# Second layer by seven products: accumulating in two banks, 4 KB operand pieces, loads placed anew

## The chip, the cores and the metric

The kernel runs on one core of one Trainium2 chip. The metric is the device time of one execution in microseconds; the time before is the median of three runs.

## The reference

Performer attention of 8 x 8 heads (576 positions, head size 64, 128 features), then a mixing layer and a two-layer MLP on the 4608 rows of 512 columns:

```python
x = attention(q, k, v, omega)            # (8, 576, 512)
u = x + ((x.transpose(0, 2, 1) @ U) @ V).transpose(0, 2, 1)
out = u + np.maximum(u @ w_ch1, 0.0) @ w_ch2   # 512 -> 2048 -> 512
```

The change touches only the last line.

## The kernel before

All products are of fp32r halves: an operand is split into a high and a low part, and one product is three matmuls (high x high, high x low, low x high).

The attention and the mixing layer come first and leave `u` in `u_dram`. The MLP then goes over six chunks of 768 rows. Chunk 0 is multiplied plainly, under the end of the mixing layer. Chunk 1 takes its first layer by Strassen-Winograd (seven products of half-size blocks in place of eight) and its second layer plainly (`second`). Chunks 2 to 5 take both layers by seven products (`products2` and `Group`).

**The first layer.** The 2048 columns of `w_ch1` make 8 pairs p of two 128-column blocks. A pair has seven slots i; the slots of a chunk are counted n = 7p + i, from 0 to 55. In slot i, `product` (L1020) multiplies the split operand `slots[i]` of the chunk (sums and differences of its blocks) by the split weights of that product into bank X (even i) or Y (odd i), six matmuls of 128 x 384. X and Y of one pair are Y and X of the next. `after(i)` combines the banks on VectorE and ScalarE into the ReLU outputs and their sums, as seven operands T[1] to T[7] of the second layer; `less` (L1066) makes low parts and differences, `both` (L1076) splits two operands at once. Operations that may wait a little stand in the lists `due` and `pend`; `flush` runs them.

**The second layer.** Two pairs make a group of four per chunk. While a group's successor runs its first layer, the group's seven products of two halves j run in 14 steps s, one in each slot (`block`, L1289: six matmuls of 128 x 384). The order within a slot is fixed by hand:

```python
self.product(i, w, (X, Y))
evict, early_due = slot(i), len(due)    # slot(i) issues the block
after(i)
if i == 0 and pend:
    pend.pop(0)()
evict()
...                                      # operations due
lowers()                                 # low parts of the next chunk's operands
between(i)                               # loads, stores, next chunk
```

Products 1 and 6 stay in banks of their own over the chunk. Products 3, 2, 5, 7 and 4 start afresh in each group, in the bank `p_m` (j = 0) or `p_kv` (j = 1), and `evict` adds each to its sum (`sums`, L816), on VectorE. The order is `ORDER = (1, 3, 2, 6, 5, 7, 4)`. In the last group products 6, 7 and 4 run on in the bank of product 1, eight evictions go into sums (some banks are added twice), and GpSimd adds the sums of products 5, 6, 7 among each other in the group before it.

**The weights.** Chunk 1 stores the split operands of the first layer into `wx_dram` (`Weights`) and of the second into `w2x_dram` (`seconds`), and chunks 2 to 5 read them again: `Again.add` loads one operand of 256 KB (`wx`, 2 KB per partition) per slot, seven slots ahead, and `Group.load` one of 256 KB (`wy`) per slot.

**The next chunk.** `forward` fetches `u` of the next chunk into `uraw` (L376: pieces of 96 KB in runs of 128 bytes), `turn` transposes it on VectorE into free columns of `w1f` (L955), `prepare` makes the sums (L806), and `add` makes one operand of the slots: ScalarE the high part (L981), VectorE the low part (L806) in the `lowers` of the slot behind it. The last three operands and `prepare(4)` follow in the new chunk (`complete`: operands 5, 6, 7 at i = 0, 2, 4).

**Output.** `Output` transposes the four sums of the chunk before (`turn`, L1340, L1344), and `write` stores them (L1350: runs of 128 bytes).

Every operation of these stages is kept in program order on its engine and in its DMA queue; nearly all DMAs are issued by SP.

Of the kernel before, what the change touches and what calls it, by code (L numbers as in the profile page):

```python
# [29 lines left out]
def performer_mlp_kernel(ctx: ExitStack, tc, q, k, v, omega, U, V, w1, w2, out):  # L30
# [790 lines left out]

    def weight_tile():
        return up.tile([P, 2, 2, P], F32R, name="wx", bufs=8)

    w2x_dram = [dram.tile([P, 7, 2, 2 * P], F32, name=f"w2x_dram{p}") for p in range(NH)]
    wx_dram = [[dram.tile([P, 2, 2, P], F32, name=f"wx_dram{p}_{i}") for i in range(7)] for p in range(NH)]

    class Weights:
# [14 lines left out]
        def add(self):  # L843
# [15 lines left out]
            keep(nc.sync.dma_start(out=wx_dram[self.p][i], in_=f32(self.ops[-1])))  # L859

    class Again:


        def __init__(self, p):
            self.p, self.ops = p, []

        def add(self):
            i = len(self.ops)
            self.ops.append(weight_tile())
            keep(nc.sync.dma_start(out=f32(self.ops[-1]), in_=wx_dram[self.p][i]))  # L870

    def seconds(p):
# [8 lines left out]
            out=w2x_dram[p][:, i : i + n, h, :], in_=x.rearrange("p (n m) -> p n m", m=2 * P)  # L881
# [39 lines left out]
    class Chunk:  # L921
# [17 lines left out]
        def total(self, i):  # L939


            if self.c > 1:
                if i == 3:
                    return self.block(0, 1)
# [13 lines left out]
        def prepare(self, i):  # L958
# [7 lines left out]
            if self.c == 1 and i < 4:  # L966
# [49 lines left out]
        def product(self, i, w, banks):  # L1016
            o, x, wt = banks[i % 2], slots[i], w.ops[i]
# [7 lines left out]
        def products(self, p, w, between, steps, spread):  # L1025
# [24 lines left out]
            for i in range(7):  # L1050
                self.product(i, w, (X, Y))
# [6 lines left out]
        def products2(self, p, w, slot, between, pend):  # L1058
# [9 lines left out]
            def one(i, x):  # L1068
                T[i] = late["tl"].tile([P, 2, HT], F32R, name=f"t{i}", bufs=2)
# [43 lines left out]
            for i in range(7):  # L1113
                self.product(i, w, (X, Y))
# [36 lines left out]
        def residual(self, t):  # L1151
            if t in ((0, 1) if self.c else (2, 3)):
                self.u[t] = dec.tile([P, DM], F32, name="u", tag="de", bufs=2)
            elif self.c:
                self.u[t] = (dec if t < 4 else late["rp"]).tile([P, DM], F32, name="u", tag="mag" if t < 4 else "u", bufs=2)
            else:
                self.u[t] = (late["rp"] if t % 2 else dec).tile([P, DM], F32, name="u", tag="u" if t % 2 else "mag", bufs=2)
# [44 lines left out]
    def each(f, i):  # L1202
# [15 lines left out]
        if f == NF - 1:  # L1218
            pairs.add()
# [20 lines left out]
    ORDER = (1, 3, 2, 6, 5, 7, 4)  # L1240
# [12 lines left out]
    def make_acc():  # L1253
        places = [parted(w1f[:, r, 1408 : 1408 + HT]) for r in range(4)]
        places += [parted(late["rp"].tile([P, DM], F32, name="acc", tag="u", bufs=2)[:, :HT]) for _ in range(2)]
        places += [w1f[:, r, :].rearrange("p (a b) -> p a b", a=2)[:, :, 768 : 768 + HT // 2] for r in range(4)]
        for i, key in enumerate([(i, j) for i in (3, 5, 2, 4, 7) for j in range(2)]):
            acc[key] = places[i]

    class Group:  # L1260


        def __init__(self, chunk, g):
            self.chunk, self.g, self.T, self.w = chunk, g, [], {}

        def load(self):
            for k, i in enumerate(ORDER):
                for n in range(2):
                    w = self.w[i, n] = late["tr"].tile([P, 2, 2 * P], F32R, name="wy", bufs=8)
                    keep(nc.sync.dma_start(out=f32(w), in_=w2x_dram[2 * self.g + n][:, PLACE[i]]))  # L1270
                    yield

        def block(self, s):

            k, j = divmod(s, 2)
            i, res, last = ORDER[k], self.chunk.res, self.g == LAST
            key = 1 if last and i in (6, 7, 4) else i
            if key in (1, 6):
                if self.g == 0:
                    res[i, j] = ps.tile([P, HT], F32, name="p_r", tag="p_n" if i == 6 else "p_q", bufs=2)  # L1280
                bank = res[key, j]
            else:
                bank = ps.tile([P, HT], F32, name="p_o", tag="p_kv" if j else "p_m")
            more = key in (1, 6) and self.g > 0
            for n in range(2):
                w, x = self.w[i, n], self.T[n][i]
                js = slice(j * P, (j + 1) * P)
                for m, (l, r) in enumerate(passes((w[:, 0, js], w[:, 1, js]), (x[:, 0], x[:, 1]))):
                    keep(nc.tensor.matmul(  # L1289
                        bank, l, r, start=(n + m == 0 and not more), stop=(n == 1 and m == 2), skip_group_check=True,  # L1290
# [3 lines left out]
        def evict(self, i, j, bank):  # L1294
            chunk = self.chunk
            a = {n: acc[n, j] for n in (2, 3, 4, 5, 7)}
            if self.g == LAST:
                for n in {1: (2,), 6: (3,), 5: (3, 5), 7: (5,)}.get(i, (i,)):
                    sums(a[n], bank, a[n], ADD)
                return  # L1300
            if i == 1:
                return
            if i == 6:
                if self.g == LAST - 1:
                    chunk.f6[j] = parted(dec.tile([P, HT], F32, name="f6", tag="mag", bufs=2))
# [200 lines left out]
```

## Time and profile before

| | us |
|---|---|
| median of 3 runs | 1117.76 |
| lowest and highest run | 1117.25, 1119.66 |
| the profiled execution: its time | 1114.54 |
| its span, first to last instruction | 1112.8 |
| TensorE busy | 1052.9 (95%) |
| VectorE busy | 786.5 (71%) |
| ScalarE busy | 605.6 (54%) |
| GpSimd busy | 516.2 (46%) |

Busy time is the time in which an instruction of the engine runs. PE is TensorE's matmuls, PEld its weight loads, DVE VectorE, ACT ScalarE, POOL GpSimd, SP SyncE. A TensorE at half clock counts as busy. Times in the trace count from the span's start. The attention and mixing end at about 311 us, chunk 0 at 439, chunk 1 at 571, chunk 2 at 695, chunk 3 at 825, chunk 4 at 959, and the products of chunk 5 at 1084.

### The profile page before, as it was taken

How to read it: one execution, taken by the hardware profiler on the slowest of the kernel's cores; microseconds unless marked ns; L12 is line 12 of the kernel's file. 1: busy time of each engine (PE TensorE's matmuls, PEld its weight loads, DVE VectorE, ACT ScalarE, POOL GpSimd, SP SyncE). 2: the span in 40 equal slices, each digit the busy share in tenths (PEclk: the TensorE clock that was granted, in tenths of full speed). 3: DMA queues.
4: the chain of work that ended last, by engine and by line, in shares of the span. 5: the costliest groups of instructions: out<-in, count | busy, mean ns of one | idle time of the engine just before them, and what ended most of it. 6: DMA issues, size and time to landing. Idle time of an engine off the chain costs nothing.

```text
span 1112.8 us, 19650 instructions
## 1 busy us (share of the span) xinstructions
PE 1052.9 (95%) x6447; PEld 1002.8 (90%) x6447; DVE 786.5 (71%) x1519; ACT 605.6 (54%) x1513; POOL 516.2 (46%) x454
## 2 busy tenths in 40 slices
PE   9999999999999999899997999799989998899995
PEld 7999999999989998799887999799978998889994
DVE  4888998989877784656746567765586555875555
ACT  5899899898856553444335434434343443434330
POOL 3447457575545555478733324422272332722352
PEclk9999999999999999899998999899999998999998
DMA  9899897995144653689686899499986999779856
GB/s 137 143 164 166 175 183 117 221 142 106 47 161 133 161 114 114 208 264 285 227 284 232 272 248 296 155 274 287 248 249 198 285 259 228 241 229 290 266 199 133
DMA packets 420773, 226.47 MB, mean 204 GB/s; under 512 B 329792, under 2 KB 344128, under 8 KB 420672
## 3 DMA queue, kind: packets, MB, share of 16 engines
q1 hardware_dynamic: 411968, 224.14, 77.6%
q10 hardware_dynamic: 8704, 1.08, 0.7%
q8 instruction: 52, 0.85, 0.3%
q14 instruction: 49, 0.40, 0.1%
HBM read 176.91 MB, written 48.23 MB: 202 GB/s over the span
## 4 chain that ended last, share of the span: by engine, by line
PE 75%; DVE 12%; DMA 5%; ACT 3%; issue 2%; SPq 2%; POOL 1%; DVEq 0%; ACTq 0%; POOLq 0%
PE p_s L1020 22%; PE p_o L1289 10%; PE p_r L1289 6%; PE p_p L993 6%; PE p_n L532 4%; PE p_kv L486 4%; PE p_n L1139 3%; PE p_q L1139 3%; PE p_p L574 3%; PE p_q L512 2%; PE p_p L575 2%; PE p_p L576 2%; DVE ux L806 2%; PE py L346 2%; DMA uraw<-u_dram 2%
## 5 line engine op out<-in xcount | busy, mean ns | idle before, releaser
L1020 PE MATMUL p_s<-ux,wx 128*128 128x384 f32 x1680 | 350.9, 344 | 41.4 <-DVE t L1066 19.7
L1020 PEld LDWEIGHTS p_s<-ux,wx 128*128 128x128 f32 x1680 | 304.1, 193 | 55.4 <-DVE t L1066 22.4
L589 ACT ACTIVATE e<-p_p,nm 128x128 f32<-128x128 f32 x576 | 167.1, 389 | 23.8 <-DVE nm L582 15.5
L1289 PE MATMUL p_o<-t,wy 128*128 128x384 f32 x864 | 173.0, 335 | 0.7 <-DVE w1f L816 0.6
L816 POOL TENSOR_TENSOR near<-b,near 128x384 f32<-128x384 f32 x32 | 43.5, 1360 | 258.7 <-DVE near L1066 258.7
L1289 PEld LDWEIGHTS p_o<-t,wy 128*128 128x128 f32 x864 | 152.1, 188 | 1.4 <-DVE w1f L816 1.3
L436 POOL TENSOR_TENSOR xl<-xT,xh 128x384 fp32r<-128x384 f32 x95 | 94.1, 1009 | 112.4 <-ACT xh L432 94.3
L582 DVE TENSOR_REDUCE nm<-p_p 128x4 f32<-128x512 f32 x144 | 97.8, 680 | 22.6 <-PE p_p L576 14.3
L1076 ACT CAST t<-near 128x768 fp32r<-128x768 f32 x64 | 53.5, 836 | 97.7 <-DVE near L1066 71.3
L816 DVE TENSOR_TENSOR w1f<-p_o,w1f 128x384 f32<-128x384 f32 x112 | 61.1, 552 | 64.4 <-PE p_o L1289 64.2
L1289 PE MATMUL p_r<-t,wy 128*128 128x384 f32 x480 | 100.0, 346 | 0.0
L574 PE MATMUL p_p<-omh,xh 128*128 128x256 f32 x288 | 92.7, 322 | 1.1 <-ACT e L589 0.9
L1289 PEld LDWEIGHTS p_r<-t,wy 128*128 128x128 f32 x480 | 89.0, 197 | 0.0
L816 DVE TENSOR_TENSOR near<-p_s,near 128x384 f32<-128x384 f32 x88 | 48.5, 551 | 50.9 <-PE p_s L1020 50.7
L575 PE MATMUL p_p<-oml,xh 128*128 128x256 f32 x288 | 81.6, 283 | 0.0
L576 PE MATMUL p_p<-omh,xl 128*128 128x256 f32 x288 | 81.5, 284 | 0.0
L816 POOL TENSOR_TENSOR t<-near,t 128x768 fp32r<-128x768 f32 x32 | 59.3, 1854 | 30.6 <-ACT t L1076 30.6
L532 PE MATMUL p_n<-kv,eT 128*128 128x65 f32 x512 | 71.2, 269 | 0.1
L993 PE MATMUL p_p<-ux,wx 128*128 128x384 f32 x384 | 70.8, 336 | 0.0
L532 PEld LDWEIGHTS p_n<-kv,eT 128*128 128x128 f32 x512 | 67.1, 192 | 2.3 <-DVE x L557 0.3
L993 PEld LDWEIGHTS p_p<-ux,wx 128*128 128x128 f32 x384 | 67.6, 188 | 1.6
L486 PE MATMUL p_kv<-vt,e 128*128 128x65 f32 x480 | 66.3, 262 | 0.7 <-ACT e L589 0.7
(175 smaller groups left out, 2206.6 us busy)
## 6 DMA issues: line engine op xcount, KB each, us to landing
wx<-wx_dram SPq DMA_DIRECT2D x224, 256.0 KB, 4.6
wy<-w2x_dram SPq DMA_DIRECT2D x224, 256.0 KB, 4.3
raw<-in_moe_w_ch_dram SPq DMA_DIRECT2D x32, 512.0 KB, 4.1
wx_dram<-wx SPq DMA_DIRECT2D x56, 256.0 KB, 2.3
u_dram<-x SPq DMA_DIRECT2D x36, 256.0 KB, 2.2
qt<-in_q_dram SPq DMA_DIRECT2D x120, 72.0 KB, 3.1
uraw<-u_dram SPq DMA_DIRECT2D x80, 96.0 KB, 5.8
kt<-in_k_dram SPq DMA_DIRECT2D x52, 144.0 KB, 5.0
```

Of the source, the lines that this page charges most:

```text
L436: rest.tensor_tensor(out=self.xl[-1], in0=self.turned, in1=f32(self.xh[-1]), op=ALU.subtract)
L486: tc.keep_in_program_order(nc.tensor.matmul(o, e[:, j, :], w, start=(s == 0 and j == 0), stop=(s == NT - 1), skip_group_check=True))
L532: nc.tensor.matmul(pn[:, h, :], eT[:, h, :], kv[:, h, s // 5, :], start=True, stop=True)
L574: nc.tensor.matmul(o, part.xh[g][:, ts], oh, start=True, stop=False)
L575: nc.tensor.matmul(o, part.xh[g][:, ts], ol, start=False, stop=False)
L576: nc.tensor.matmul(o, part.xl[g][:, ts], oh, start=False, stop=True)
L582: nc.vector.tensor_reduce(out=self.nm[:, :n], in_=self.pp[:, :n], axis=AX.X, op=ALU.max, negate=True)
L589: nc.scalar.activation(out=self.e[:, j, :], in_=self.pp[:, j, :], func=AF.Exp, bias=self.nm[:, j : j + 1])
L816: keep(engine.tensor_tensor(out=out, in0=a, in1=b, op=op))
L993: keep(nc.tensor.matmul(ph, l, r, start=(cc + i == 0), stop=(cc == NC - 1 and i == 2)))
L1020: keep(nc.tensor.matmul(o, l, r, start=(i in (0, 1, 3) and k + j == 0), stop=(k == 1 and j == 2), skip_group_check=True,))
L1289: keep(nc.tensor.matmul(bank, l, r, start=(n + m == 0 and not more), stop=(n == 1 and m == 2), skip_group_check=True,))
```

## The change

- The order is `(1, 5, 2, 6, 3, 7, 4)`. Per half j, products 1, 6, 7 and 4 of a group go on accumulating in one bank (`p_q`) and products 5 and 3 in another (`p_m` or `p_kv`); product 2 stays in its bank (`p_n`) over the chunk. After each product but 2 the bank is added to one sum as it stands: after 1 to sum 2, after 6 to sum 3, after 7 and 5 to sum 5, after 3 to sum 3, after 4 to sum 4. Product 2 is added in the last group. The additions on GpSimd, the copies of products 6 and 7 and the double additions of the last group go. The first group adds the chunk's own blocks.
- The sums have new places, sum 5 two of them, used in turn by chunk.
- `wx_dram` is one tensor, from which two operands are loaded at once (`feed`: 512 KB, 4 KB per partition, every other slot, six slots ahead); `w2x_dram` holds both pairs of a group side by side, so that a `wy` load is 512 KB as well.
- `forward` begins at slot 20 in place of 30 and turns at 29, 33, 38, 42 in place of 36, 40, 44, 48; the first four operands are made at 50, 51, 52, 55 in place of 50, 52, 53, 55, the rest at 0, 1, 2 in place of 0, 2, 4; `prepare(4)` runs in slot 53 in place of slot 1, on GpSimd. In chunk 1 the operands of chunk 2 are made in slots 50 to 55, so that one is left.
- In chunk 1, chunk 0's stores come in slots 4 to 9, its seventh weights in slot 0, its last operand at i = 3. The first two residual tiles of chunk 1 have tag `uraw` in place of `de`.
- The output leaves as two tiles of 768 rows (sums 2 and 3) and four of 384 (sums 4 and 5), in other slots; at the end each sum is written when it is complete.

```diff
+    def weight_pair():
+        return up.tile([P, 2, 2, 2, P], F32R, name="wx", bufs=4)
...
-        return up.tile([P, 2, 2, P], F32R, name="wx", bufs=8)
+        if not halves:
+            pair = weight_pair()
+            halves.extend([pair[:, 0], pair[:, 1]])
+        return halves.pop(0)
...
+    w2x_dram = [dram.tile([P, 7, 2, 2, 2 * P], F32, name=f"w2x_dram{g}") for g in range(NH // 2)]
+    wx_dram = dram.tile([P, 7 * NH, 2, 2, P], F32, name="wx_dram")
...
-            if self.c == 1 and i < 4:
+            if self.c == 1 or i == 4:
                 sums(to, a, b, SUBTRACT, nc.gpsimd)
...
-            if t in ((0, 1) if self.c else (2, 3)):
+            if self.c and t < 2:
+                self.u[t] = late["rp"].tile([P, TOK], F32, name="uraw", bufs=2)[:, :DM]
+            elif not self.c and t in (2, 3):
                 self.u[t] = dec.tile([P, DM], F32, name="u", tag="de", bufs=2)
...
-    ORDER = (1, 3, 2, 6, 5, 7, 4)
+    ORDER = (1, 5, 2, 6, 3, 7, 4)
...
+        def load(self, s):
+            k, odd = divmod(s + 6, 2)
+            if odd or not 0 <= k < 7:
+                return
+            i = ORDER[k]
+            self.w[i] = late["tr"].tile([P, 2, 2, 2 * P], F32R, name="wy", bufs=4)
+            keep(nc.sync.dma_start(out=f32(self.w[i]), in_=w2x_dram[self.g][:, PLACE[i]]))
...
+            if i == 1:
+                self.banks[i, j] = ps.tile([P, HT], F32, name="p_c", tag="p_q", bufs=2)
+            elif i == 5:
+                self.banks[i, j] = ps.tile([P, HT], F32, name="p_o", tag="p_kv" if j else "p_m")
+            elif i == 2 and self.g == 0:
+                self.chunk.res[j] = ps.tile([P, HT], F32, name="p_r", tag="p_n", bufs=2)
+            bank = self.chunk.res[j] if i == 2 else self.banks[5 if i in (5, 3) else 1, j]
+            fresh = i in (1, 5) or i == 2 and self.g == 0
...
         def evict(self, i, j, bank):
+            if i == 2 and self.g < LAST:
                 return
+            a = sum_of(self.chunk.c, {1: 2, 6: 3, 7: 5}.get(i, i), j)
+            first_of = {1: (0, 0), 5: (1, 1), 6: (0, 1), 4: (1, 0)}
+            if self.g == 0 and i in first_of:
+                sums(a, bank, parted(self.chunk.block(*first_of[i])[:, j]), ADD)
             else:
+                sums(a, bank, a, ADD)
...
+    def feed(s):
+        q = s + 6
+        if q % 2 == 0 and q < 7 * NH * (NCH - 2):
+            pair = weight_pair()
+            keep(nc.sync.dma_start(out=f32(pair), in_=wx_dram[:, q % (7 * NH) : q % (7 * NH) + 2]))
+            wq[q], wq[q + 1] = pair[:, 0], pair[:, 1]
...
-                    forward(nxt, n, ((30, 34, 38, 42), (36, 40, 44, 48), (42, 49, 50), ADDS))
+                    forward(nxt, n, ((20, 24, 30, 34), (29, 33, 38, 42), (35, 43, 44), ADDS))
+                    if n == 53:
+                        nxt.prepare(4)
...
+    ADDS, REST = (50, 51, 52, 55), (0, 1, 2)
```

## Rows read from the trace of the kernel before

**Rows 1.** Timeline, undisturbed, chunk 2: start, us, instruction, [idle before]

```profile
644.96 1.20 PE L1020 MATMUL p_s<-ux,wx 128*128 128x384 f32 x6
646.20 0.56 DVE L816 TENSOR_TENSOR near<-p_s,near 128x384 f32<-128x384 f32 x1 [0.48 <-PE p_s L1020]
648.33 0.55 DVE L816 TENSOR_TENSOR acc<-p_o,acc 128x384 f32<-128x384 f32 x1
649.31 0.96 DVE L816 TENSOR_TENSOR t<-near,t 128x768 fp32r<-128x768 f32 x1 [0.44 <-ACT t L1076]
650.19 0.55 DVE L1066 SCALAR_TENSOR_TENSOR t<-p_s,t 128x384 fp32r<-128x384 f32 x1
651.20 1.03 PE L1020 MATMUL p_s<-ux,wx 128*128 128x384 f32 x5
```

**Rows 2.** Timeline of TensorE, chunks 2 to 5

```profile
607.39 1.32 PE L1020 MATMUL p_s<-ux,wx 128*128 128x384 f32 x6 [1.77 <-DVE t L1066]
701.52 1.31 PE L1020 MATMUL p_s<-ux,wx 128*128 128x384 f32 x6 [3.94 <-DVE t L1066]
716.72 1.97 PE L1020 MATMUL p_s<-ux,wx 128*128 128x384 f32 x5 [2.75 <-DVE ux L806]
831.65 1.50 PE L1020 MATMUL p_s<-ux,wx 128*128 128x384 f32 x6 [3.94 <-DVE t L1066]
928.87 2.29 PE L1020 MATMUL p_s<-ux,wx 128*128 128x384 f32 x6 [3.59 <-DVE t L1066]
965.23 1.90 PE L1020 MATMUL p_s<-ux,wx 128*128 128x384 f32 x6 [3.97 <-DVE t L1066]
1083.43 1.20 PE L1289 MATMUL p_o<-t,wy 128*128 128x384 f32 x6
```

**Rows 3.** Busy times by stretch; the last three columns: clock, DMA share, GB/s

```profile
929.00:935.00 6.00, 6.00 (x19) 6.00 (x20) 1.71 (x3) 1.04 (x2) 0.00 (x0) 0.50 1.13 225
```

**Rows 4.** Waits of TensorE from 437 us on: total us, times, longest

```profile
PE p_s L1020 <- DVE t L1066: 19.7, 8, 4.0
```

**Rows 5.** Timeline of VectorE at the change from chunk 2 to 3

```profile
693.72 0.55 DVE L816 TENSOR_TENSOR near<-p_s,near 128x384 f32<-128x384 f32 x1
...
695.12 1.25 DVE L1066 SCALAR_TENSOR_TENSOR near<-near 128x384 f32<-128x384 f32 x1
...
698.04 1.28 DVE L806 SCALAR_TENSOR_TENSOR ux<-w1f,ux 128x768 fp32r<-128x768 f32 x1
...
715.37 1.29 DVE L806 SCALAR_TENSOR_TENSOR ux<-w1f,ux 128x768 fp32r<-128x768 f32 x1
```

**Rows 6.** Groups by line, GpSimd: xcount | busy us, mean ns | idle before

```profile
L816 POOL TENSOR_TENSOR t<-near,t 128x768 fp32r<-128x768 f32 x32 | 59.3, 1854 | 30.6 <-ACT t L1076 30.6
L816 POOL TENSOR_TENSOR w1f<-w1f 128x384 f32<-128x384 f32 x24 | 32.1, 1344 | 0.8
```

**Rows 7.** Timeline of VectorE, slot 48 of chunk 2

```profile
684.20 1.04 DVE L955 STREAM_TRANSPOSE w1f<-uraw 128x384 f32<-128x384 f32 x2 [2.77 <-DMA uraw<-u_dram]
```

**Rows 8.** DMA issues: xcount, KB each, median us to landing

```profile
wx<-wx_dram SPq DMA_DIRECT2D x224, 256.0 KB, 4.6
uraw<-u_dram SPq DMA_DIRECT2D x80, 96.0 KB, 5.8
```

**Rows 9.** Timeline of TensorE and VectorE, starts of chunks 1 and 2

```profile
455.96 1.97 PE L1020 MATMUL p_s<-ux,wx 128*128 128x384 f32 x5 [3.44 <-DVE ux L806]
581.37 1.22 PE L1020 MATMUL p_s<-ux,wx 128*128 128x384 f32 x6
583.30 0.56 DVE L816 TENSOR_TENSOR b<-p_s,near 128x384 f32<-128x384 f32 x1 [5.89 <-DMA out_dram<-u]
592.69 11.88 PE L1020 MATMUL p_s<-ux,wx 128*128 128x384 f32 x53 [2.36 <-DVE ux L806]
```

**Rows 10.** Busy times by stretch, at the end

```profile
1094.00:1098.00 4.00, 4.00 (x25) 4.00 (x24) 3.96 (x9) 0.00 (x0) 0.00 (x0) 1.00 0.16 59
1102.00:1106.00 4.00, 0.00 (x0) 0.00 (x0) 0.98 (x4) 0.00 (x0) 0.00 (x0) 0.96 0.92 137
```

More of the change, by code (lines that the diff above doesn't have):

```diff
@@ L1218, in each @@
         if f == NF - 1:
-            pairs.add()
             while nxt.made < NC:
@@ L1260, in performer_mlp_kernel, with sum_of @@
+    def sum_of(c, i, j):
+        return acc[(i, j, c % 2) if i == 5 else (i, j)]
     class Group:
         def __init__(self, chunk, g):
[L1264 to L1271, printed above, removed]
+            self.chunk, self.g, self.T, self.w, self.banks = chunk, g, [], {}, {}
+        def load(self, s):
[5 more added lines that the diff above has]
+            keep(nc.sync.dma_start(out=f32(self.w[i]), in_=w2x_dram[self.g][:, PLACE[i]]))
@@ L1273, in block @@
         def block(self, s):
             k, j = divmod(s, 2)
[L1276 to L1284, printed above, removed]
+            i = ORDER[k]
@@ L1289, in block @@
                     keep(nc.tensor.matmul(
-                        bank, l, r, start=(n + m == 0 and not more), stop=(n == 1 and m == 2), skip_group_check=True,
+                        bank, l, r, start=(fresh and n + m == 0), stop=(n == 1 and m == 2), skip_group_check=True,
                     ))
@@ new lines, in write_out, with whole_room, half_room @@
+    def write_out(c, i, j, a, y, engine=nc.sync):
+        r, n = first[c] * P + (i in (3, 5)) * HT, y.shape[-1]
+        k = ((i > 3) * 2 + j) * P + a * BLK
+        keep(engine.dma_start(
+            out=rows_out[r : r + n, k : k + BLK].rearrange("(b i) j -> i b j", i=BLK),
+            in_=y[a * BLK : (a + 1) * BLK, :].rearrange("i (b j) -> i b j", j=BLK),
+        ))
+    def whole_room():
+        return late["rp"].tile([P, TOK], F32, name="uraw", bufs=2)
+    def half_room(n):
+        return const.tile([P, DM], F32, name="yh", tag=f"w2{'hl'[n % 2]}{n // 2}")[:, :HT]
@@ L1410, in performer_mlp_kernel @@
                 group = Group(now, p // 2)
-            else:
-                loads = group.load()
-            new = Again((p + 1) % NH) if p + 1 < NH or nxt else None
             def slot(i):
@@ L1425, in between @@
                 n = 7 * p + i
-                next(loads, None)
-                if new:
-                    new.add()
-                if c == 2 and n in (0, 2, 5, 8, 12, 14):
-                    stores.pop(0)()
-                if p == 0:
-                    complete(now, i)
-                if c > 2:
-                    if n in (10, 11, 20, 21):
-                        m = (10, 11, 20, 21).index(n)
-                        ys[m] = Output(c - 1, m)
-                        for t in range(2):
-                            ys[m].turn(t)
-                    for m, b in enumerate((12, 16, 22, 26)):
-                        if b <= n < b + 4:
-                            ys[m].write(n - b)
@@ L1442, in between @@
-                if nxt:
-                    forward(nxt, n, ((30, 34, 38, 42), (36, 40, 44, 48), (42, 49, 50), ADDS))
-            group.T.append(now.products2(p, pairs, slot, between, pend))
-            pairs = new
+                feed(7 * NH * (c - 2) + n)
+                if p % 2:
+                    group.load(i - 7)
+                elif done:
+                    done.load(i)
+                if c == 2:
+                    if n in (0, 3, 6, 9, 11, 13):
+                        stores.pop(0)()
+                    if n == 0:
+                        now.add()
+                elif n in REST:
+                    now.add()
@@ L1447, in performer_mlp_kernel @@
+            at = 7 * NH * (c - 2) + 7 * p
+            group.T.append(now.products2(p, lambda i: wq.pop(at + i), slot, between, pend))
             if p % 2:
@@ L1452, in performer_mlp_kernel, with end @@
         pend.pop(0)()
+    def end(i, j, y):
+        turn_out(NCH - 1, i, j, y)
+        for a in range(4):
+            write_out(NCH - 1, i, j, a, y, nc.scalar if j else nc.sync)
     ys = {}
```

181 lines of the change are left out of this document (72 added, 109 removed).

## Prediction

> **What bounds the kernel now.** The table of times says that TensorE is busy 95% of the span. That share is no answer: an array at half clock counts as busy, and the view of waits and the order of time show where the rest goes. I read the waits of TensorE from 437 us on (the stage with seven products per pair), then its timeline, then VectorE beside it.
>
> An undisturbed slot is 2.08 us: six matmuls of the first layer and six of the second, 1.04 us each. From the product that starts at 644.96 to the one at 651.20 there are three such slots, 6.24 us, back to back [rows 1]. A chunk has 56 slots, so 116.5 us. The rows of TensorE that begin with a wait give what a chunk takes [rows 2]: the second product of chunk 3 starts at 701.52, of chunk 4 at 831.65, of chunk 5 at 965.23. So chunk 3 takes 130.13 us and loses 13.65; chunk 4 takes 133.58 and loses 17.1. Chunk 2, from slot 15 (607.39) to the same place (701.52), takes 94.13 for 42 slots of 87.4 and loses 6.8. Chunk 5, from 965.23 to its last block at 1083.43, takes 118.2 for 54 slots and one product, 113.4, and loses 4.8. Together 42.4 us. [...]
>
> Who ends the waits: mostly VectorE's L1066 [rows 4]. This instruction reads bank X after product 6, and product 1 of the next pair writes that bank. In the undisturbed slots VectorE takes the sum of product 5 at 646.20, three more instructions, an eviction, a sum of 768 columns and L1066, which ends at 650.74; the product follows at 651.20. The margin is 0.46 us, and VectorE itself idles 0.43 us between the eviction's end (648.88) and that sum, which waits for ScalarE until 649.31 [rows 1]. So about 0.9 us of extra work between slot 5 and slot 6 is free, and anything more stops TensorE.
>
> What exceeds it is of two kinds. First, at each change of chunk the same sequence runs from 693.72 to about 701.5, 7.7 us in place of 4.5 [rows 5]: a split of the next chunk (1.28 us) lies in it, and instructions of 0.56 us take 1.25 us while GpSimd adds accumulators (24 additions of 1344 ns in all at this form [rows 6]). Five slots later a second wait comes: 2.75 us at 716.72, for the split that starts at 715.37, of the slot operand that product 6 needs; it is made at i = 4 and split at i = 5, behind the sums of product 5 [rows 2, 5]. Second, a transpose of `uraw` waits in VectorE's queue for its DMA (2.77 us at 684.20 [rows 7]) and holds up all behind it; the wait of 3.59 us in chunk 4 is of this kind [rows 2].
>
> **The change, part by part.**
>
> *Loads of the next chunk.* The pieces of `uraw` are fetched from slot 20 on and turned at 29, 33, 38, 42; the last piece is issued five or six slots ahead of its turn, 10.4 to 12.5 us, where it was three, 6.2 us. A piece lands 5.8 us after issue at the median [rows 8], so three slots were just short where SP or the queue was late, and five leave 4.6 us. I take the whole of the second kind as gone. The turn at 33 stands in slot 5 of an even pair, which now has no eviction (the block is product 2's): 1.04 us in place of 0.47 and the 0.43 of idling, within the margin. If it is contended it costs up to 0.7 us a chunk.
>
> *Change of chunk.* The splits move to slots 50, 51, 52, 55 and 0, 1, 2 of the next chunk: none is left in slots 5 and 6 of the last pair, and that for product 6 is done by slot 3, three slots early. The ten GpSimd additions per chunk go (13.4 us of GpSimd, by 1344 ns). `prepare(4)` goes from VectorE to GpSimd, in slot 53: an instruction of 768 columns, 1.85 us by the row of that shape [rows 6]. It starts behind the split of slot 52, some 1.6 us after product 5 starts, and so lies beside the first two of the three instructions of 0.56 us. By the row at 695.12 that costs 0.7 us each [rows 5], and the first sum starts 0.3 us late: 1.0 to 1.7, less the margin of 0.46, so 0.7 us stays of each change (0.5 to 1.2).
>
> That row shows only that two such instructions slow each other. [...]
>
> *Banks.* Products 1, 6, 7, 4 run on in one bank per half and 5, 3 in another, and each product but the second is added from its bank into the sums. That is 12 evictions a group and 14 in the last, 50 a chunk, where the code before has 44: six more of 0.55 us, 3.3 us of VectorE a chunk; two small transposes more and four ScalarE copies less change nothing. VectorE idles more than that. New is that product 4's bank must be read before product 1 of the next group writes it, two slots later. The eviction of slot 12 would end where that of the row at 648.33 ends, 648.88, and the next group's block starts 1.04 us ahead of the product at 651.20, at 650.16 [rows 1]: 1.28 us to spare. That of slot 13 comes behind L1066, so at 651.3, and its block starts at 652.24: 0.9 us to spare. So nothing in undisturbed slots; at a change of chunk L1066 decides first.
>
> *4 KB pieces.* TensorE never waited for `wx` or `wy`, so larger pieces take nothing from the path. Half the issues on SP and the same bytes help only the queue before `uraw`.
>
> *Sum for chunks 2 to 5.* Of the 42.4 us I let 2 stay in each of chunks 2 to 4 (0.7, and 1.3 for turns and waits that are not seen here) and 1 in chunk 5: 35.4 gained. Bounds: 42.4, and 25 if half of the changes' loss stays.
>
> *Start of chunk 1.* Product 6 waits 3.44 us for a split and its next matmuls run at half clock (1.97 us for five) [rows 9]. The split moves one slot earlier, and five stores of chunk 0, which VectorE did between slots 0 and 5, begin at slot 4. I take 5.5 gained: 3.44, the wait just before it, and some 1.1 of clock. Bounds 2 (the stores and splits then crowd slots 4 to 6) and 7.
>
> *From chunk 1 to 2.* VectorE's sum `b` waits 5.89 us for a store of `u`, because both have tag `de`; now rows 0 and 1 go to `uraw`. Later product 6 waits 2.36 us for a split, then made two slots before [rows 9]. With both gone: product 2 starts at 581.37 as now, five products later the next pair starts at 586.6. There no second-layer block covers the sequence of VectorE, so product 1 of the second pair waits: the 1.77 us of the row at 607.39 [rows 2] and the missing block, 2.8 in all, a wait that the late split hides today. Then product 1 of the third pair starts at about 590.4 + 6.2 + 2.1 + 1.8, so 600.6, in place of 607.39. That is 6.8; with a chance of half clock I take 6 (4 to 7).
>
> *End.* From 1102 us the DMA engines are 92% busy with the output at 137 GB/s, while from 1094 to 1098 they are 16% busy [rows 10]. A quarter of the last chunk's 1.57 MB, 2.9 us at that rate, is now written as soon as sum 2 is complete, four blocks earlier. I take 2.5 (0 to 3; zero if the eight more issues bound it).
>
> Sum: 35.4 + 5.5 + 6 + 2.5 = 49.4. The profiled execution took 1114.54 us for its span of 1112.8; it would take 1065.1. The median shown, 1117.76, lies 3.2 above it; I keep that distance: 1068.4, so 1068 us.
>
> **The rivals.**
>
> *Transposes still late.* In favour: the loads of weights keep their bytes, and 24 slots in a row carry small pieces. Against: five slots of lead. Then the second kind stays: 6.8 less the change of chunk leaves about 1 in chunk 2, 3 in chunk 3, 7 in chunk 4: 11 us, 1079. Chance 0.10.
>
> *The change of chunk stays crowded.* In favour: four splits still fall on slots 50 to 55, and GpSimd now works beside VectorE in slot 53. If the wait of 3.94 us and its half clock stay, some 5 us three times: 1083. Chance 0.12.
>
> *Slower: 512 KB loads land too late.* A pair of `wx` operands is now issued six slots ahead, 12.5 us, in one piece, often beside a `wy` piece of the same size. A piece of 256 KB lands 4.6 us after issue [rows 8]; one of 512 KB between 4.6 and 9.2, under 12.5. It decides only above that: chunks 2 to 5 read 112 pairs, and each that lands later than 12.5 us stops TensorE by the excess. At 12.95 us the gain of 49 is spent; at 13.15 the kernel takes some 23 us more than now, 1141. Chance 0.06.
>
> *No change.* The waits go over to GpSimd's `prepare(4)` and to the evictions, one for one: 1118. Chance 0.03.
>
> **How the numbers follow.** The forecast has 0.69. Its own range is 1056 (all bounds at their good end) to 1078. The range 1056 to 1086 takes in the two rivals that gain less, and leaves out about 0.15. Less than 0.2% is what a measurement of this kernel cannot tell from no change. Faster: 0.69 + 0.10 + 0.12, 0.91; same 0.03; slower 0.06.
>
> **What would show it.** Right: slots of 2.08 us throughout chunks 3 to 5 and a period of about 118.5 us; no wait of VectorE for `uraw`; no split among slots 5 and 6 of the last pair; waits of TensorE for L1066 under 1 us at the changes of chunk, with a granted clock at the upper level; at the second pair of chunk 2 a wait near 2.8 us that is new. Wrong: waits of products for `wx` or of blocks for an eviction, or VectorE's queue longer in slots 53 to 57 than now.

## The result and the profile after

| | before | after |
|---|---|---|
| median of the runs beside each other, us | 1118.71 | 1067.90 |
| lowest to highest, us | 1117.25 to 1120.51 | 1065.40 to 1070.19 |
| ratio, 95% interval | | 0.9545 (0.9516 to 0.9573) |
| span of the profiled execution, us | 1112.8 | 1065.2 |

The change makes the kernel 50.8 us faster; forecast were 49.4 us and a time of 1068. In the kernel after, product's matmul is L1017 (was L1020), the block's L1293 (was L1289), `less` is L1063 (was L1066) and the transpose of `uraw` L952 (was L955).

The waits of TensorE from 437 us on (total us, times, longest), which answer to [rows 4]:

```profile
PE p_s L1017 <- DVE t L1063: 6.4, 5, 2.8
PE p_c L1293 <- DVE w1f L816: 1.9, 4, 1.0
PE p_s L1017 <- DVE ux L806: 1.1, 1, 1.1
...
PE p_c L1293 <- DMA wy<-w2x_dram: 0.8, 1, 0.8
```

The wait for `less` falls from 19.7 to 6.4 us. New are waits of blocks for an eviction: 0.30 us at each of the three changes of chunk, and 1.0 us in the last group, where the kernel before waited 0.6. Two of the five waits for `less` stand at the start of chunk 2 (2.80 and 1.77 us), where the blocks of the second layer have not begun or only just begun; three stand at the changes of chunk. TensorE's timeline shows the first of them and the change from chunk 2 to 3, against 3.94 us of [rows 2]:

```profile
585.82 9.16 PE L1017 MATMUL p_s<-ux,wx 128*128 128x384 f32 x42 [2.80 <-DVE t L1063]
...
685.67 1.21 PE L1017 MATMUL p_s<-ux,wx 128*128 128x384 f32 x6
687.18 1.32 PE L1293 MATMUL p_c<-t,wy 128*128 128x384 f32 x6 [0.30 <-DVE w1f L816]
689.09 1.33 PE L1017 MATMUL p_s<-ux,wx 128*128 128x384 f32 x6 [0.60 <-DVE t L1063]
690.26 1.20 PE L1293 MATMUL p_c<-t,wy 128*128 128x384 f32 x6
```

From 685.67 to 690.26 three groups of six matmuls take 4.59 us in place of 3 x 1.04, so the change loses 1.47 us. The granted clock is 1.00 there (687 to 694 us).

To see where the 47.6 us between the two spans went, I cut each profiled execution at the same products, read from TensorE's timeline. Times in us; "chunk 2" runs from its slot 15 to slot 1 of chunk 3, chunks 3 and 4 from slot 1 to the next chunk's slot 1, chunk 5 from slot 1 to the end of the last block, the tail from there to the end of the span. 56 undisturbed slots are 116.5, the stretch of chunk 2 is 87.4. The columns of before and after differ by 47.9 in all, because chunk 1 starts some 0.4 us later in the kernel after.

| | chunk 1, slots 0 to 15 | to chunk 2, slot 15 | chunk 2 | chunk 3 | chunk 4 | chunk 5 | tail |
|---|---|---|---|---|---|---|---|
| before | 38.0 | 129.9 | 94.1 | 130.1 | 133.6 | 135.2 | 12.3 |
| after | 32.5 | 125.4 | 91.3 | 117.9 | 118.0 | 130.5 | 9.7 |
| `after_again` | 32.5 | 125.2 | 90.3 | 117.9 | 117.9 | 130.5 | 9.2 |
| `three_edges` | 37.2 | 128.9 | 90.4 | 118.4 | 118.7 | 130.5 | 12.1 |
| `old_sums` | 32.5 | 124.2 | 92.2 | 125.3 | 120.6 | 132.0 | 9.4 |
| `late_splits` | 32.5 | 125.0 | 88.9 | 121.9 | 123.9 | 133.5 | 9.2 |
| `late_loads` | 32.5 | 125.3 | 93.1 | 118.4 | 120.2 | 130.5 | 9.2 |
| `two_kb_late` | 32.5 | 125.4 | 91.4 | 120.8 | 121.4 | 130.5 | 9.4 |
| `old_body` | 33.4 | 125.3 | 93.8 | 127.0 | 131.4 | 137.9 | 9.8 |
| `loads_splits` | 33.4 | 126.2 | 91.1 | 122.9 | 122.9 | 135.1 | 9.2 |
| `sums_splits` | 33.3 | 124.6 | 92.3 | 128.2 | 127.0 | 133.6 | 9.2 |
| `prepare_again` | 32.5 | 125.7 | 87.5 | 116.6 | 116.5 | 130.5 | 9.2 |

### The profile page after: what moved, and what is told of

Its sections match the earlier page's. It is cut to its first block, busy times and chain, and to the rows that moved or that the text cites. A ratio compares the mean times of both kernels' runs of the same rounds, so it can differ in the third digit from the quotient of the medians.

```text
span 1065.2 us, 19235 instructions
## 1 busy us (share of the span) xinstructions
PE 1036.5 (97%) x6447; PEld 990.4 (93%) x6447; DVE 785.2 (74%) x1546; ACT 600.8 (56%) x1497; POOL 478.5 (45%) x419
## 4 chain that ended last, share of the span: by engine, by line
PE 86%; DVE 7%; ACT 3%; DMA 2%; issue 1%; POOL 1%; DVEq 0%; SPq 0%; ACTq 0%; POOLq 0%
PE p_s L1017 24%; PE p_c L1293 11%; PE p_o L1293 6%; PE p_p L990 6%; PE p_kv L486 4%; PE p_n L532 4%; PE p_n L1136 4%; PE p_q L1136 4%; PE p_p L574 3%; PE p_r L1293 3%; PE p_p L575 3%; PE p_p L576 3%; PE p_q L512 2%; PE py L346 2%; PE p_kv L1136 2%; PE p_m L1136 2%
## 5 line engine op out<-in xcount | busy, mean ns | idle before, releaser
L1017 PE MATMUL p_s<-ux,wx 128*128 128x384 f32 x1680 | 338.9, 337 | 8.8 <-DVE t L1063 6.4
L1017 PEld LDWEIGHTS p_s<-ux,wx 128*128 128x128 f32 x1680 | 297.9, 189 | 17.3 <-DVE t L1063 8.0
L1293 PE MATMUL p_c<-t,wy 128*128 128x384 f32 x768 | 153.6, 335 | 3.3 <-DVE w1f L816 1.9
L436 POOL TENSOR_TENSOR xl<-xT,xh 128x384 fp32r<-128x384 f32 x95 | 94.1, 1010 | 112.9 <-ACT xh L432 91.6
L1293 PEld LDWEIGHTS p_c<-t,wy 128*128 128x128 f32 x768 | 134.6, 188 | 5.2 <-DVE w1f L816 3.2
L1293 PE MATMUL p_o<-t,wy 128*128 128x384 f32 x384 | 76.5, 334 | 0.0
L816 POOL TENSOR_TENSOR t<-near,t 128x768 fp32r<-128x768 f32 x32 | 61.7, 1930 | 31.2 <-ACT t L1073 31.2
L1293 PEld LDWEIGHTS p_o<-t,wy 128*128 128x128 f32 x384 | 67.5, 188 | 0.0
L183 POOL TENSOR_TENSOR mag<-mag,low 128x512 int32<-128x512 int32 (+2 forms) x35 | 45.3, 1295 | 46.2 <-DVE mag L161 42.6
```

The source lines that it names most:

```text
L816: keep(engine.tensor_tensor(out=out, in0=a, in1=b, op=op))
L1017: keep(nc.tensor.matmul(o, l, r, start=(i in (0, 1, 3) and k + j == 0), stop=(k == 1 and j == 2), skip_group_check=True,))
L1293: keep(nc.tensor.matmul(bank, l, r, start=(fresh and n + m == 0), stop=(n == 1 and m == 2), skip_group_check=True,))
```

## The experiments

Each is the kernel after with the edit shown. The theory is the prediction's: the gain comes from where splits, evictions, loads and stores stand in VectorE's queue. `after_again` is the measure:

> The kernel after, unchanged, on the same chip as the three kernels above, as the measure for them. Both theories: 1066 to 1070 us, ratio to the kernel before 0.952 to 0.957, and the two splits of the time the same as before to 1 us: chunk periods of 117.95 us, tail 9.7 us.

Measured: 1066.19 us, ratio 0.9559 (0.9539 to 0.958), with chunks 3 and 4 at 117.9 us. Single executions of one kernel differ by up to 7 us, those of the kernel before by up to 9. What an experiment costs is given below by medians; the ratios, each to the kernel before on the same chip, give the same within 3 us.

**1. The sums as before** (`old_sums`).

```diff
-    ORDER = (1, 5, 2, 6, 3, 7, 4)
+    ORDER = (1, 3, 2, 6, 5, 7, 4)
...
+                if i == 5:
+                    pool(a[5], chunk.f6[j])
+                    pool(a[3], a[5])
```

> The second layer as in the kernel before (order 1, 3, 2, 6, 5, 7, 4, fresh banks, GpSimd adding the sums, 44 evictions a chunk) with everything else as after: loads, splits, 512 KB pieces, output. Theory of placement (the gain of chunks 2 to 5 comes from when loads and splits are placed): the ten GpSimd additions slow VectorE at three changes of chunk by 2 to 4 us each, so 1074 to 1080 us against 1068. Rival of the banks (running on in two banks is what saves): most of the gain goes, above 1095 us.

Measured: 1075.49 us, 0.9627 (0.9589 to 0.9665). That is 8 to 9 us more than the kernel after, in the range of the placement theory. At each change product 1 waits 2.77 us, and behind the first of these waits six matmuls take 2.06 us in place of 1.20:

```profile
688.73 1.34 PE L1017 MATMUL p_s<-ux,wx 128*128 128x384 f32 x6 [2.77 <-DVE t L1063]
689.90 2.06 PE L1293 MATMUL p_r<-t,wy 128*128 128x384 f32 x6
```

What lengthens VectorE's queue there is GpSimd. The instruction of VectorE at 683.17, with 384 columns and both operands in SBUF, ends 0.42 us after the GpSimd instruction that was under way (683.17 + 1.26 = 684.43 against 682.68 + 1.33 = 684.01), while the eviction at 685.64, which reads one of its operands from a bank, takes its usual 0.54 us beside the next:

```profile
682.68 1.33 POOL L816 TENSOR_TENSOR w1f<-w1f 128x384 f32<-128x384 f32 x1
...
685.26 2.13 POOL L816 TENSOR_TENSOR w1f<-w1f 128x768 f32<-128x768 f32 x1
```

```profile
683.17 1.26 DVE L1063 SCALAR_TENSOR_TENSOR near<-near 128x384 f32<-128x384 f32 x1
...
685.64 0.54 DVE L816 TENSOR_TENSOR w1f<-p_o,w1f 128x384 f32<-128x384 f32 x1
```

The edit takes back banks, order and evictions together with GpSimd's additions; the additions were not tried alone.

VectorE also waited 2.21 us (chunk 2) and 4.08 us (chunk 3) for pieces of `uraw` in this execution, though they are fetched from slot 20 on. Behind the longer one TensorE does not wait until the change. But TensorE itself waits in chunk 3 for weights, 1.20 us for `wx` and 0.44 for `wy`, and part of the 125.3 us is that: neither the early loads nor the six slots of lead are proof against a crowded stretch.

```profile
778.61 1.28 PE L1017 MATMUL p_s<-ux,wx 128*128 128x384 f32 x6 [1.20 <-DMA wx<-wx_dram]
```

**2. The splits as before** (`late_splits`; `prepare(4)` stays on GpSimd, in slot 1).

```diff
-    ADDS, REST = (50, 51, 52, 55), (0, 1, 2)
+    ADDS, REST = (50, 52, 53, 55), (0, 2, 4)
...
-                    if n == 53:
-                        nxt.prepare(4)
+                    if n == 1:
+                        now.prepare(4)
```

> After, with only the splits of the next chunk back: operands at 50, 52, 53, 55 and 0, 2, 4, prepare(4) in slot 1 of the next chunk, still on GpSimd. Theory of placement: the wait of product 6 for its split returns at each of three changes, 2.75 us and about 1.5 us of half clock, and the split of slot 53 lies in slot 5 again: 11 to 15 us, 1079 to 1083 us. Rival (with GpSimd's additions gone VectorE has room for them): at most 3 us more, below 1071.

Measured: 1077.95 us, 0.9663 (0.9626 to 0.9699), 10 to 12 us more than the kernel after: at or just under the low end. But the edit also takes `prepare(4)` out of slot 53, which by itself gains some 4 us (experiment 6). Against `prepare_later`, which ran beside it and has `prepare(4)` in slot 1 too, on VectorE, the late splits cost 1077.95 - 1063.02 = 14.9 us, the upper end of what was expected. On which engine it runs there does not show in TensorE's waits: `loads_splits`, with VectorE, has the same for splits and for `less` (8.3 us each). The wait of product 6 of [rows 2] is back at its old size at all three changes, with 1.24 us before it:

```profile
686.56 1.32 PE L1017 MATMUL p_s<-ux,wx 128*128 128x384 f32 x6 [1.24 <-DVE t L1063]
...
700.18 1.14 PE L1017 MATMUL p_s<-ux,wx 128*128 128x384 f32 x5 [2.75 <-DVE ux L806]
```

**3. The loads of `u` as before** (`late_loads`).

```diff
-  forward(nxt, n, ((20, 24, 30, 34), (29, 33, 38, 42), (35, 43, 44), ADDS))
+  forward(nxt, n, ((30, 34, 38, 42), (36, 40, 44, 48), (42, 49, 50), ADDS))
```

> After, with only the fetches and turns of the next chunk (and the sums made from them) back at the slots of before: fetched from 30, turned at 36, 40, 44, 48. Theory of placement: transposes wait for their DMA again, 8 to 11 us in chunks 2 to 4, 1076 to 1079 us, with VectorE waiting for uraw. Rival of the pieces (4 KB pieces and half the issues make the DMA queue fast enough): no wait for uraw, within 2 us of 1068.

Measured: 1070.84 us, 0.9586 (0.955 to 0.9623): 3 to 5 us, between the two. The transposes do wait again, but in this execution 3.20 us at one of them cost TensorE nothing and 3.42 at the next (which the profile puts down to a `wx` load) cost it 1.30:

```profile
666.07 1.04 DVE L952 STREAM_TRANSPOSE w1f<-uraw 128x384 f32<-128x384 f32 x2 [3.20 <-DMA uraw<-u_dram]
677.12 1.04 DVE L952 STREAM_TRANSPOSE w1f<-uraw 128x384 f32<-128x384 f32 x2 [3.42 <-DMA wx<-wx_dram]
...
679.99 1.31 PE L1017 MATMUL p_s<-ux,wx 128*128 128x384 f32 x6 [1.30 <-DVE b L816]
```

**4. Pieces of 256 KB** (`two_kb`, and with the late loads `two_kb_late`).

```diff
-            keep(nc.sync.dma_start(out=f32(pair), in_=wx_dram[:, q % (7 * NH) : q % (7 * NH) + 2]))
+            for k in range(2):
+                keep(nc.sync.dma_start(out=f32(pair[:, k]), in_=wx_dram[:, q % (7 * NH) + k]))
```

(`wy` in the same way.)

> The kernel after, with each 512 KB load of a pair of `wx` operands or of a pair of `wy` operands issued as two loads of 256 KB (2 KB per partition) in the same slots. Theory (placement: the gain comes from where splits, loads and stores stand, and the size of the pieces is worth nothing): 1066 to 1070 us, within 2 us of the kernel after, and no wait of TensorE for `wx` or `wy` over 1 us. Rival (pieces: half as many issues on SP leave room for the rows of `u`, and that is where part of the gain comes from): 1073 us or more, with VectorE again waiting for `uraw` or TensorE for `wx`. The same run with the loads of `u` late (next one) says whether the small pieces cost more there.

> The same 256 KB loads, and the rows of `u` fetched from slot 30 on and turned at 36, 40, 44, 48 as in the kernel before. In 512 KB pieces those late loads cost some 5 us of the 11 that the prediction gave them. Theory (size of pieces worth nothing there too): 1070 to 1074 us, and VectorE's transposes wait for `uraw` no longer than 1 us in all. Rival (the old cost came from late loads behind twice as many issues): 1076 us or more, with waits of VectorE for `uraw` near the 2.8 to 3.6 us of the kernel before.

Measured: 1066.3 us, 0.9549 (0.9533 to 0.9565), and 1073.95 us, 0.9616 (0.9595 to 0.9637). With early loads the size of the pieces is worth nothing. With late loads 7.8 us are lost instead of 3 to 5, but the intervals of the two ratios overlap (0.9595 to 0.9637, and 0.955 to 0.9623 for `late_loads`), so that a worth of some 3 us is not shown. The time lies in the range of the theory; the waits are those of the rival. VectorE's waits at L952 are 12.9 us in all, all for `uraw`, against 11.9 in `late_loads` (8.5 for `uraw`, 3.4 put down to a `wx` load). The longest is this one, with what it costs TensorE:

```profile
916.70 1.04 DVE L952 STREAM_TRANSPOSE w1f<-uraw 128x384 f32<-128x384 f32 x2 [4.18 <-DMA uraw<-u_dram]
...
919.57 1.32 PE L1017 MATMUL p_s<-ux,wx 128*128 128x384 f32 x6 [1.54 <-DVE b L816]
```

The prediction's sentence that half the issues help only the queue before `uraw` is not borne out: `uraw` lands in 4.8 us at the median in `two_kb_late` and in 5.1 in `late_loads`. As a cause of the gain the larger pieces do nothing, because the time with early loads is the same.

**5. Three edges** (`three_edges`): the first split and the stores of chunk 1, the residual's tag, the writes at the end.

```diff
-                if 4 <= n < 10 or n >= 10 and stores:
+                if stores:
...
-            if self.c and t < 2:
-                self.u[t] = late["rp"].tile([P, TOK], F32, name="uraw", bufs=2)[:, :DM]
-            elif not self.c and t in (2, 3):
+            if t in ((0, 1) if self.c else (2, 3)):
...
-            write_out(NCH - 1, i, j, a, y, nc.scalar if j else nc.sync)
+            write_out(NCH - 1, 2 if i == 3 else i, j, a, y if z is None else z, nc.scalar if a % 2 else nc.sync)
```

> The kernel after with three edits undone that stand in three different stretches, to be read by place and not by the total alone: (1) the first operands and the stores of chunk 0 stand where the kernel before has them at the start of chunk 1, (2) rows 0 and 1 of chunk 1's residual go to tag `de` again, (3) the last chunk's output is written as in the kernel before. Theory (each edit gives what the prediction says, and they add): slot 15 of chunk 1 comes 5 to 5.5 us later than in the kernel after, slot 15 of chunk 2 10 to 11.5 us later, the tail behind the last matmul is 12.3 us in place of 9.7, and the time is 1079 to 1082. Rivals, each by its own mark: the start is set by the bank scheme and the first loads (slot 15 of chunk 1 less than 2 us later); the store under `de` is hidden (slot 15 of chunk 2 no later than slot 15 of chunk 1 already was); the tail was bound by the number of writes (no difference there).

Measured: 1078.07 us, 0.9656 (0.9642 to 0.9671), 11.9 us more than the kernel after beside it, 1 us under the range. In the table: 4.7 us in chunk 1, 3.5 on the way to chunk 2, 2.4 in the tail. Slot 15 of chunk 1 comes 5.2 us later, as expected, slot 15 of chunk 2 8.8 us later, less than the 10 expected. The waits of [rows 9] are back in their places (3.44 and 5.89 us there):

```profile
455.75 1.97 PE L1017 MATMUL p_s<-ux,wx 128*128 128x384 f32 x5 [3.45 <-DVE ux L806]
...
585.13 0.56 DVE L816 TENSOR_TENSOR b<-p_s,near 128x384 f32<-128x384 f32 x1 [5.22 <-DMA out_dram<-u]
```

**6. What is left at the changes** (`prepare_later`, and again with more rounds `prepare_again`): `prepare(4)` of chunks 3 to 5 on VectorE, in slot 1 of its chunk.

```diff
-            if self.c == 1 or i == 4:
+            if self.c == 1 or i == 4 and self.c == 2:
                 sums(to, a, b, SUBTRACT, nc.gpsimd)
...
+                    if n == 1:
+                        now.prepare(4)
```

> After, with prepare(4) of chunks 3 to 5 moved from GpSimd in slot 53 to VectorE in slot 1 of the next chunk; splits as after. If the 1.23 us that TensorE still loses at each change of chunk come from a VectorE instruction that waits while GpSimd runs prepare(4): the row of 1.95 us goes back to 0.56, the loss falls to at most 0.3 us each, 3 us less in all, about 1065. If they come from the splits in slots 51 to 53: no change, 1068.

> The kernel after with `prepare(4)` of chunks 3 to 5 on VectorE in slot 1 of its chunk, again, in more rounds. If GpSimd's 1.84 us instruction in slot 53 held VectorE: no wait of TensorE at any change of chunk, 1061 to 1064 us, ratio to the kernel before 0.950 to 0.953, below that of the kernel after (0.9545 and 0.956). If the first run was chance: 1066 to 1068.

Measured: 1063.02 us, 0.9522 (0.9491 to 0.9553), and 1061.64 us, 0.9514 (0.9489 to 0.9539). In the second execution chunks 3 and 4 take 116.6 and 116.5 us, 56 undisturbed slots to 0.1 us, and after the start of chunk 2 one wait of 1.0 us is left. It was not timed beside the kernel after; by medians it gains 3 to 6 us on it, with intervals of the ratios that overlap. The traces say the same: chunks 3 and 4 take 1.4 us less each, 4.2 for three changes. (In the first execution chunk 3 still took 118.2, with waits of 0.48 us for a `wx` and 0.64 for a `wy` load in it.) The cause is seen on GpSimd and VectorE in the kernel after:

```profile
683.22 1.84 POOL L816 TENSOR_TENSOR w1f<-w1f 128x768 f32<-128x768 f32 x1 [7.28 <-DVE ux L806]
```

```profile
683.52 1.95 DVE L1063 SCALAR_TENSOR_TENSOR t<-near,t 128x384 fp32r<-128x384 f32 x1
685.50 0.56 DVE L1063 SCALAR_TENSOR_TENSOR near<-near 128x384 f32<-128x384 f32 x1
686.10 0.56 DVE L1063 SCALAR_TENSOR_TENSOR near<-near,b 128x384 f32<-128x384 f32 x1
686.57 0.55 DVE L816 TENSOR_TENSOR w1f<-p_c,w1f 128x384 f32<-128x384 f32 x1
```

and in `prepare_again`, where GpSimd has nothing there:

```profile
682.56 0.55 DVE L1063 SCALAR_TENSOR_TENSOR t<-near,t 128x384 fp32r<-128x384 f32 x1
683.15 0.56 DVE L1063 SCALAR_TENSOR_TENSOR near<-near 128x384 f32<-128x384 f32 x1
683.74 0.56 DVE L1063 SCALAR_TENSOR_TENSOR near<-near,b 128x384 f32<-128x384 f32 x1
```

The instruction of 0.56 us that starts 0.30 us behind GpSimd's ends at 685.47, 0.41 us after GpSimd's end at 685.06; it takes 1.39 us more, and the next is quick again (0.56 us). Why it lasts until then is not shown.

The kernel before has the same: the row at 695.12 of [rows 5] ends at 696.37, 0.42 us after this instruction of GpSimd.

```profile
694.75 1.20 POOL L816 TENSOR_TENSOR w1f<-w1f,f 128x384 f32<-128x384 f32 x1
```

**7. Do the parts add up?** (`old_body`: experiments 1, 2, 3 and the 256 KB pieces together; `loads_splits` and `sums_splits`: pairs. All with `prepare(4)` on VectorE in slot 1, as before.)

```diff
-    ORDER = (1, 5, 2, 6, 3, 7, 4)
-    ADDS, REST = (50, 51, 52, 55), (0, 1, 2)
-  forward(nxt, n, ((20, 24, 30, 34), (29, 33, 38, 42), (35, 43, 44), ADDS))
+    ORDER = (1, 3, 2, 6, 5, 7, 4)
+    ADDS, REST = (50, 52, 53, 55), (0, 2, 4)
+  forward(nxt, n, ((30, 34, 38, 42), (36, 40, 44, 48), (42, 49, 50), ADDS))
```

> The kernel after with everything of chunks 3 to 5 as in the kernel before: old scheme of the sums, splits in slots 50, 52, 53, 55 and 0, 2, 4 with `prepare(4)` on VectorE in slot 1, rows of `u` fetched from slot 30 on, 256 KB loads. The start of chunk 1, the step from chunk 1 to 2 and the tail stay as in the kernel after. Undone one at a time, the sums cost 9 us, the splits 11, the loads of `u` 5 (7 with 256 KB pieces). Theory (separate stretches, undoing them all adds up): 1066.5 + 9 + 11 + 7 = 1093 us, 1090 to 1096, with chunk 3 and 4 at about 126 us each. Rival (one queue: all three lengthen VectorE's queue around the change of chunk, and each costs more when the others have used up the slack): 1102 to 1107, the time before less the 12.3 us that the three edges measured, with chunk 3 near 130 and chunk 4 near 133 us.

> The kernel after with two of the three undone: the late splits with `prepare(4)` on VectorE in slot 1, and the late loads of `u` in 512 KB pieces. Separate stretches: 1066.5 + 11 + 5 = 1082 us (1080 to 1085). One queue: 1087 or more, with the late transpose at slot 48 and the splits from slot 50 on seen as one wait at the change of chunk that is longer than 1.5 us.

> The kernel after with the other pair undone: old scheme of the sums (with GpSimd's ten additions at the change of chunk) and the late splits with `prepare(4)` on VectorE in slot 1. Separate stretches: 1066.5 + 9 + 11 = 1086 us (1084 to 1089). One queue: 1092 or more, the wait for L1063 at each change longer than the sum of the two alone (2.9 and 1.4 us). A third outcome, that both share one wait and the sum is less: under 1082.

Measured: `loads_splits` 1084.9 us, 0.9713 (0.9691 to 0.9734), 1084.9 - 1066.2 = 18.7 us more than the kernel after; `sums_splits` 1089.2 us, 0.9742 (0.972 to 0.9764), 23.0 us more. The first lies at the upper end of what was given for separate stretches, the second just above it; neither reaches the one-queue figure. `old_body` 1101.64 us, 0.9865 (0.984 to 0.989): 35.4 us more, between the two theories and just under the second. In these three runs `prepare(4)` of chunk 1 goes to VectorE as well, which the expectations did not count: chunk 1 takes 0.8 to 0.9 us more in the table. The one-queue effect exists: the wait at the change is 2.98 us in `sums_splits` and 3.94, as in [rows 2], once the late loads are added:

```profile
690.11 1.21 PE L1017 MATMUL p_s<-ux,wx 128*128 128x384 f32 x5 [2.98 <-DVE t L1063]
```

```profile
692.31 1.01 PE L1017 MATMUL p_s<-ux,wx 128*128 128x384 f32 x2 [3.94 <-DVE t L1063]
```

`old_body` exceeds the sum of its parts by 6.4 us by medians (9 + 12 + 8 = 29), and 0.9 of that is chunk 1. Most of it comes in with the late loads: `old_body` is `sums_splits` with the late loads and the 256 KB pieces added, and takes 1101.64 - 1089.2 = 12.4 us more beside it, where the same two edits cost 7.8 alone. One us at each of three changes is 3 of it. Single executions differ by as much as the rest, so that stays open.

`old_body` and `three_edges` together undo 35.4 + 11.9 = 47.3 us of the 51. The output's new slots in chunks 3 to 5 were not undone in any run.

## Why the prediction was right, and where its steps were not

**The body of chunks 2 to 5.** Forecast 35.4 us gained. In the table chunk 2 gives 2.8, chunk 3 12.2, chunk 4 15.6 and chunk 5 4.7: 35.3; undoing it all in `old_body` costs 35.4 by medians (0.9 of it in chunk 1) and 32.4 in these four columns. The period of 118.5 us was 117.9. The mechanism is right: what stood in VectorE's queue stopped TensorE. That the sum agrees to 0.1 us is luck: the forecast gave 4.8, 11.7, 15.1 and 3.8 for the four chunks, and they miss it by -2.0, +0.5, +0.5 and +0.9. The parts are less right than the sum:

- *Loads.* The second kind of wait was put at 11 us. The transposes of the kernel after indeed wait for no piece of `uraw`. But undone alone, the late loads cost 3 to 5 us, 8 with 256 KB pieces; on top of the old sums and late splits they cost 12.4. The step that failed is to give them a price of their own: a late transpose costs only what exceeds the slack of the product waiting behind it, and with the old splits and sums little of that slack is left. The rival with these transposes still late is out.
- *Change of chunk, splits and sums.* Splits 10 to 12 us (14.9 with `prepare(4)` in slot 1 on either side) and sums 8 to 9 us, each with its own wait (2.75 us for the split before product 6, 2.77 for L1063). The prediction took both as one loss at each change and was right that it goes. The rival with the change still crowded would have kept waits near 3.94 us; they are 0.30 and 0.60.
- *`prepare(4)` on GpSimd.* The term was 0.7 us of each change, from two instructions that would take 0.7 us more each. Measured: one instruction takes 1.39 us more, and each change loses 1.47 us, above the term's own bound of 1.2. The row at 695.12 of [rows 5] was misread as a fixed surcharge of 0.7 us. It ended 0.42 us after GpSimd's instruction of 1.20 us, and beside one of 1.84 us that had started 0.30 us earlier VectorE's instruction likewise ended 0.41 us after GpSimd's, and so took 1.95 us.
- *Banks.* No undisturbed slot waits, as worked out. The clause that L1066 decides first at a change was wrong: the block of product 1 waits first, 0.30 us, for the eviction of slot 12, which the instruction of 1.95 us delays too. Blocks that wait for an eviction were one of the prediction's signs of being wrong; that sign has come, at this small price.
- *Rest.* Chunks 3 and 4 keep 1.5 us where 2 were left: 0.7 for `prepare(4)` was half of what it cost, and nothing came of the 1.3 for turns and waits not seen, so two errors nearly cancel. Chunk 5 gains 0.9 more than given, and chunk 2 keeps 3.9 where 2 were left. Beside the 1.5 of the change it waits 0.81 us for a `wy` piece, 0.66 and 0.19 us for VectorE; `prepare_again` shows 87.5 us there, so these come and go.

**Start of chunk 1.** Forecast 5.5, measured 38.0 - 32.5 = 5.5, of which `three_edges` gives back 4.7. Here too two errors cancel. TensorE's waits in this stretch fall from 5.3 to 2.0 us, by 3.3 and not by the 4.5 of the sum, because it now waits 1.1 us for another split and 0.9 for ScalarE; the other 2.2, which go with the granted clock of 0.50 that the kernel before shows from 456 to 460 us, were put at 1.1.

**From chunk 1 to 2.** Forecast 6, measured 4.5. The new wait of 2.8 us is there, and the 1.77 us of [rows 2] stays. One mis-sized term is the clock, for which 0.8 of the 6.8 us were taken off: behind the 2.80 us the granted clock falls to 0.50. The windows behind either wait (the last three columns as in [rows 3]):

```profile
587.00:589.00 2.00, 2.00 (x8) 2.00 (x8) 0.56 (x1) 0.93 (x3) 1.82 (x1) 0.50 0.86 234
598.00:601.00 3.00, 3.00 (x18) 3.00 (x18) 1.45 (x3) 1.89 (x3) 1.98 (x2) 1.00 0.84 279
```

Eight matmuls in 2 us at a granted clock of 0.50 stand against eighteen in 3 us at 1.00, behind the wait of 1.77 us. In `old_sums` and `prepare_later` the same 2.80 us are followed by eighteen matmuls in 3.47 and 3.46 us, and the stretch takes 124.2 and 124.3 us in place of 125.4. So the clock costs some 1.1 us in one execution and nothing in another; it belongs into the range, not into the sum. The other mis-sized term is the path itself: without the slower clock 5.7 us are gained, not 6.8. In `prepare_later` product 1 of the third pair starts 10.9 us after that of the second, where the prediction added up 6.2 + 2.1 + 1.8 = 10.1; what the 0.8 are made of stays open.

**End.** Forecast 2.5, measured 12.3 - 9.7 = 2.6; `three_edges` brings 12.1 back.

**The range.** The good ends of the bounds add up to 42.4 + 7 + 7 + 3 = 59.4, so 1058, not the 1056 that the prediction gives for them; the outcome lies inside either.

**Slower by late 512 KB loads.** The median landing is 4.7 and 5.2 us, at the lower end of the 4.6 to 9.2 allowed, and the six slots of lead (12.5 us) were enough in this execution but for one load in chunk 2:

```profile
wx<-wx_dram SPq DMA_DIRECT2D x112, 512.0 KB, 4.7
wy<-w2x_dram SPq DMA_DIRECT2D x112, 512.0 KB, 5.2
uraw<-u_dram SPq DMA_DIRECT2D x80, 96.0 KB, 6.5
```

The `uraw` row has grown from 5.8 [rows 8], and to more than the 6.2 us that three slots give: its pieces land later, and the longer lead covers it. The one late load is in the chain of work that ended last (start, us), as a step of 10.44 us from its issue to the block at 657.49 that waited 0.81 us for it; the median hid it. The lead was not 12.5 us: the load left SP 9.8 us before the block's turn (656.68), because the issues ahead of it were late (last rows below).

```profile
646.92 10.44 DMA wy<-w2x_dram
```

Such waits come up in other executions with 512 KB pieces, 0.6 us for `wx` and 0.3 for `wy` in `after_again`, while `two_kb` has none. So the rival's mechanism exists, at about 1 us in place of the 49 that it needed; a product that waits for `wx` was a sign of being wrong.

## What to carry to other kernels

Price a schedule edit from the undisturbed slot and the measured period: what each stretch loses, less a remainder, held here to 2 us a chunk, though the split into causes did not. A price found by undoing one edit depends on what else stands in the queue: the late loads cost 3 to 8 us alone and 12 on top of the others. Before two engines' work is put side by side, look how long the instruction is that the other will meet: here a VectorE instruction of 0.56 us, with both operands in SBUF, took 1.95 us and ended 0.41 us after the GpSimd instruction of 1.84 us that it met, and the profile shows that as a longer instruction, not as idle time. An off-path instruction moved to an engine that "has time" can cost more than leaving it where it is, in a slot with slack: putting it back was worth some 4 us here.

## What the runs showed of the hardware that was not expected

A load of twice the size landed nearly as soon: 512 KB at 4.7 and 5.2 us after issue in the median, 256 KB in `two_kb` at 4.5 and 4.7, and the kernel takes the same 1066 us with either.

In chunk 2 of the kernel after, the DMA share is 1.13 and 1.12, and issues on SP take longer (those of weights below 0.69 to 1.52 us, against 0.34 in chunk 3):

```profile
620.00:640.00 20.00, 20.00 (x117) 20.00 (x116) 13.72 (x26) 8.22 (x16) 5.84 (x4) 1.00 1.13 254
640.00:660.00 20.00, 18.34 (x103) 17.38 (x102) 13.23 (x25) 7.62 (x15) 8.28 (x5) 1.00 1.12 253
720.00:760.00 40.00, 40.00 (x233) 40.00 (x232) 25.42 (x50) 15.77 (x29) 11.39 (x8) 1.00 1.13 285
```

```profile
640.52 0.69 SPq L1353 DMA_DIRECT2D wx<-wx_dram  x1
641.31 0.69 SPq L1275 DMA_DIRECT2D wy<-w2x_dram  x1
642.10 3.74 SPq L376 DMA_DIRECT2D uraw<-u_dram  x2
...
646.92 1.52 SPq L1275 DMA_DIRECT2D wy<-w2x_dram  x1
...
728.93 0.34 SPq L1275 DMA_DIRECT2D wy<-w2x_dram  x1
```

Two issues of `uraw` take 3.74 us, and the next loads of weights leave SP that much later; the row at 646.92 is the load that came late. The share alone does not explain it: in chunk 3, from 720 to 760 us, the share is the same, and loads of weights are issued in 0.34 us. What lengthens the issues stays open.
